# Output product of a pair of tiles by seven block products, transposed, in an attention and two-MLP kernel

## The chip, the cores and the metric

One core of a Trainium2 chip runs the whole program. The metric is device time in microseconds; lower is better. Engines are named as the profile names them: PE is the matrix engine (PEld its weight loads), DVE, ACT and POOL are the vector, scalar and GpSimd engines, SP issues all DMAs of this kernel from one queue, in order.

## What is computed

```python
def _attn_ref(q, k, v):
    ...
    attn = np.exp(scores)
    attn = attn / (np.sum(attn, axis=-1, keepdims=True) + 1e-09)
    return np.matmul(attn, v).astype(np.float32)

def _moe_ref(x, w_in, w_out, s, b):
    h = x @ w_in
    r = np.maximum(h, 0.0)
    g = s * (r * r) + b
    return (g @ w_out).astype(np.float32)

def _moe2_ref(x, w1, w2, w3, w_out):
    a = x @ w1
    b = x @ w2
    h = a * b @ w3
    return (h @ w_out).astype(np.float32)
```

Causal attention with a window of 128 (4 batches, 8 heads, 576 positions, head size 64) is followed by a first MLP (512 to 2048 to 512) and a second (512 to 1024, 1024 to 1024 to 512), over 2304 tokens, all in float32. Only the second MLP is touched by the change.

## The kernel before

Tokens are worked in six tiles of 384 (TT). Activations stand transposed, features on partitions and tokens along the free axis. A float32 matmul is made of three matmuls on rounded halves: each operand is split into a high part (an ACT copy to fp32r) and a low part (a subtraction), and `PASSES` runs high x high, high x low and low x high. `split_to` (line 624) is that split.

The program has these stages. Attention and the first MLP run interleaved over the six tiles (`slot`, line 983), and leave the second MLP's input x of every tile in DRAM (`x2d`, line 590). During the last tile of the first MLP, and behind it, three things are got ready:

- `w_chunk` (line 637) decodes the weights w1 and w2, eight chunks of 128 features, and builds seven left factors a chunk: A11, A12, A22, S1 to S4. Each is split and kept in SBUF, in the pool `wp` (34 buffers of 512 KB), until the end.
- `x_steps` (line 794) builds the right factors of the first pair of tiles: B11, B21, T1, T2, T4, B22, T3.
- `w3_unit` (line 595) multiplies w3 by the output weights, as these two have nothing between them: 8 steps j, each of 24 matmuls of 512 columns, into all eight PSUM banks; the weights come by `late_load` (line 1090). `w3_out` (line 607) evicts the eight banks, split, as `w3o`.

The last stage is the loop over three pairs of tiles (line 1137). `pair_chunk` (line 902) makes, for one chunk c, a and b of both tiles by seven block products instead of eight (Winograd's form of Strassen's method: rows are the chunk of w1 and that of w2, the inner axis is cut in two, columns are the two tiles). Each product (`prod`, line 831) is 6 matmuls of 384 columns. Sums are formed by `keep_copy` (ACT, line 843) and additions on DVE (lines 911, 924, 926, 928); the elementwise product a*b of the first tile is made on DVE (line 927) and that of the second on POOL (line 933). `p_split` (line 848) splits a product.

`out_mm` (line 868) is the output product: for each of the three 128-token blocks of a tile, 3 matmuls of 512 columns a chunk, accumulated over the eight chunks. The first tile's out_mm of chunk c-1 stands in the middle of chunk c:

```python
        u2 = keep_copy(u, gp, "r")
        if c:
            out_mm(2 * q, c - 1, p1s.pop())
            step()
```

and the second tile's eight stand after the pair's chunks, in one run of 72 matmuls with the first tile's last 9. Meanwhile `x_later` (line 737) builds the right factors of the next pair, a part at each `step()`, and stores them to DRAM; `x_fetch` (line 784) loads them all, 14 tiles of 384 KB, when a pair's chunks are done.

Order: a scheduler places instructions by priority (their order in the program) as operands and buffers come free, ahead of time; after that each engine runs its list in order. `tc.keep_in_program_order` holds marked instructions to the order of the program. A pool gives a tile the first buffer that is free, and the tile's first writer waits for the last reader of that buffer. Each DMA on SP also waits for the DMA eight places earlier.

## Time and profile before

| | us |
|---|---|
| median of 3 runs | 862.23 (862.08 to 874.1) |
| the profiled execution | 864.67 |
| its span | 862.8 |
| PE busy in the span | 854.9 |
| DVE busy | 571.8 |
| ACT busy | 496.5 |
| POOL busy | 344.0 |

The span is what the profiler saw from the first to the last instruction; the execution's own time is a little longer. Busy time of PE counts matmuls that overlap in the array, so it is not PE at its peak; the pitch of matmuls in a row says more.

### The profile page before, as it was taken

What the parts mean: (1) busy time and instruction counts of PE and PEld (TensorE: products, weight loads), DVE (VectorE), ACT (ScalarE), POOL (GpSimd) and SP (SyncE); (2) the same over time, 40 slices, a digit from 0 to 9 for tenths busy, and PEclk for the clock granted to TensorE, in tenths of its full rate; (3) what the DMA queues carried; (4) which work ended last, traced back from release to release, by engine and by line L of the source; (5) the groups of instructions that cost most, each with busy time, mean ns of one, the idle gap of its engine ahead of it and who ended that gap; (6) DMA issues with size and microseconds to landing.
All of it is one profiled execution on the core that took longest, in us unless ns stands there. A gap on an engine that the chain in (4) does not pass through costs nothing.

```text
span 862.8 us, 13636 instructions
## 1 busy us (share of the span) xinstructions
PE 854.9 (99%) x4676; PEld 777.4 (90%) x4676; DVE 571.8 (66%) x1186; ACT 496.5 (58%) x1180; POOL 344.0 (40%) x361
## 2 busy tenths in 40 slices
PE   9999999999999999999999999999999999999998
PEld 5766667999999999999999999889998999889996
DVE  5989997777878888778863998355544455333233
ACT  5777769877867777777764676343333334222222
POOL 0135457788666677666751302531111011101110
PEclk9999999999999999999999999999999999999999
DMA  9746513112354455445423577832428443610001
GB/s 335 284 175 213 211 60 106 55 55 85 113 167 163 163 165 197 168 155 165 135 98 119 169 268 271 312 116 83 153 86 311 147 156 120 257 73 1 1 1 74
DMA packets 51621, 129.10 MB, mean 150 GB/s; under 512 B 5984, under 2 KB 21600, under 8 KB 51552
## 3 DMA queue, kind: packets, MB, share of 16 engines
q1 hardware_dynamic: 51552, 128.23, 43.0%
q8 instruction: 37, 0.61, 0.3%
q14 instruction: 32, 0.26, 0.1%
HBM read 95.70 MB, written 32.51 MB: 149 GB/s over the span
## 4 chain that ended last, share of the span: by engine, by line
PE 89%; DVE 3%; ACT 3%; issue 2%; POOL 1%; DMA 1%; POOLq 0%; DVEq 0%; ACTq 0%; SPq 0%
PE acc L566 17%; PE hp L514 17%; PE oacc L876 12%; PE d L837 12%; PE u L837 9%; PE w3a L601 5%; PE acc L560 4%; PE hp L505 4%; PE pv L440 3%; PE s L310 2%; PE s L311 1%; PE s L305 1%; PE tp L387 1%; PE s L78 1%; PE xo L420 1%
## 5 line engine op out<-in xcount | busy, mean ns | idle before, releaser
L514 PE MATMUL hp<-x,w 128*128 128x384 f32 x960 | 185.7, 339 | 0.0
L514 PEld LDWEIGHTS hp<-x,w 128*128 128x128 f32 x960 | 167.3, 188 | 0.3
L566 PE MATMUL acc<-gh,w 128*128 128x384 f32 x640 | 125.9, 339 | 0.0
L933 POOL TENSOR_TENSOR p<-mc 128x384 f32<-128x384 f32 (+2 forms) x30 | 30.9, 1037 | 234.2 <-DVE mc L928 221.0
L566 PEld LDWEIGHTS acc<-gh,w 128*128 128x128 f32 x640 | 109.0, 188 | 0.6 <-ACT gh L535 0.3
L837 PE MATMUL d<-xb,wblk 128*128 128x384 f32 x576 | 107.9, 335 | 0.0
L837 PEld LDWEIGHTS d<-xb,wblk 128*128 128x128 f32 x576 | 101.2, 188 | 2.0
L403 POOL TENSOR_SCALAR_AFFINE_SELECT pt<-pp 128x768 fp32r<-128x768 f32 x80 | 79.0, 1010 | 31.0 <-PE pv L440 17.0
L876 PE MATMUL oacc<-w3o,ph 128*128 128x512 f32 x270 | 84.8, 395 | 0.0
L837 PE MATMUL u<-xb,wblk 128*128 128x384 f32 x432 | 83.6, 335 | 0.0
L272 POOL TENSOR_TENSOR kb<-qkraw,ka 128x512 fp32r<-128x512 f32 x40 | 57.4, 1435 | 58.7 <-ACT ka L271 58.3
L837 PEld LDWEIGHTS u<-xb,wblk 128*128 128x128 f32 x432 | 75.6, 188 | 0.9 <-ACT mc L845 0.6
L324 DVE CUSTOM_DVE_ANT_0 ns<-s,relm_sb 128x256 f32<-128x256 f32 (+1 forms) x144 | 53.3, 411 | 33.8 <-PE s L311 23.2
L368 POOL TENSOR_SCALAR pr<-pr,sm 128x128 f32<-128x128 f32 x90 | 45.5, 521 | 65.0 <-ACT z L150 20.6
L566 PE MATMUL acc<-gl,w 128*128 128x384 f32 x320 | 69.5, 337 | 1.3 <-DVE gl L543 1.3
L543 DVE TENSOR_TENSOR gl<-r,gh 128x384 fp32r<-128x384 f32 x80 | 57.3, 716 | 11.4 <-ACT gh L535 10.1
L924 DVE TENSOR_TENSOR mc<-d,mc 128x384 f32<-128x384 f32 x24 | 13.3, 556 | 76.4 <-PE d L837 76.4
L525 ACT ACTIVATE r<-hp 128x384 f32<-128x384 f32 x96 | 46.6, 485 | 25.3 <-PE hp L514 22.7
L845 ACT ACTIVATE mc<-d 128x384 f32<-128x384 f32 x48 | 23.6, 492 | 63.1 <-PE d L837 63.0
L876 PEld LDWEIGHTS oacc<-w3o,ph 128*128 128x128 f32 x270 | 50.4, 188 | 10.4
L347 ACT ACTIVATE pr<-pr,mn 128x128 f32<-128x128 f32 x120 | 46.9, 392 | 19.8 <-DVE pr L333 19.6
L566 PEld LDWEIGHTS acc<-gl,w 128*128 128x128 f32 x320 | 56.5, 188 | 1.7 <-DVE gl L543 1.6
(127 smaller groups left out, 1677.9 us busy)
## 6 DMA issues: line engine op xcount, KB each, us to landing
qkraw<-qk SPq DMA_DIRECT2D x40, 448.0 KB, 3.3
late<-st SPq DMA_DIRECT2D x23, 512.0 KB, 3.5
w<-late SPq DMA_DIRECT2D x23, 512.0 KB, 5.7
raw<-w_in SPq DMA_DIRECT2D x16, 512.0 KB, 6.5
raw<-w_out SPq DMA_DIRECT2D x16, 512.0 KB, 6.3
wr<-w SPq DMA_DIRECT2D x16, 512.0 KB, 4.1
st<-w3T SPq DMA_DIRECT2D x15, 512.0 KB, 3.8
xs<-x2d SPq DMA_DIRECT2D x32, 192.0 KB, 2.6
```

Of the source, the lines that this page charges most:

```text
L272: nc.gpsimd.tensor_tensor(out=kl, in0=k_r, in1=k.bitcast(F32), op=ALU.subtract)
L324: nc.vector.tensor_tensor_reduce(out=n[:, i, cs], in0=dst[i][:, cs], in1=relm_sb[:, VARIANT.get(t * NB + i, 0), cs], scale=2.0 ** -(h + 1) ...
L347: nc.scalar.activation(out=e[:, i, :], in_=e[:, i, :], func=AF.Exp, scale=-1.0, bias=mn[:, i:i + 1], accum_out=sm[:, i:i + 1],)
L368: nc.gpsimd.tensor_scalar(out=e[:, i, :], in0=e[:, i, :], scalar1=sm[:, i:i + 1], scalar2=1.0, op0=ALU.mult, op1=ALU.mult,)
L403: nc.gpsimd.affine_select(out=o[:, :, :, e, :], in_=pp.bitcast(F32), pattern=[[0, 2], [0, NB], [sign, P]], compare_op=op, fill=0.0, base=0 ...
L514: nc.tensor.matmul(out=hp, lhsT=wi[c][:, l, k * P:(k + 1) * P], rhs=xT[t, k][:, r, :], start=(n == 0), stop=(n == 3 * KD - 1),)
L525: chain(t * NC1 + c, nc.scalar.activation(out=rt[:, :TT], in_=hps.pop((t, c)), func=AF.Relu))
L543: nc.vector.tensor_tensor(out=gl, in0=rt[:, :TT], in1=gh.bitcast(F32), op=ALU.subtract)
L566: nc.tensor.matmul(out=x2acc[m], lhsT=wo[c][:, l, ms], rhs=g[r], start=(c == 0 and n == 0), stop=(c == NC1 - 1 and n == 2),)
L601: nc.tensor.matmul(out=accs[i], lhsT=w3g[i // 4, j][:, l, i % 4 * P:(i % 4 + 1) * P], rhs=wo2s[j][:, r, :], start=(j == 0 and n == 0), sto ...
L837: tc.keep_in_program_order(nc.tensor.matmul(out=dst, lhsT=w[:, l, ks], rhs=xblk[bnm, k][:, r, :], start=(start and n == 0), stop=(n == 5), ...
L876: tc.keep_in_program_order(nc.tensor.matmul(out=oacc[t, i], lhsT=p[l][:, cs], rhs=w3o[c][:, r, :], start=(c == 0 and n == 0), stop=(c == N ...
```

## The change

The output product is made transposed, features on partitions and the tokens of both tiles along the free axis, by seven block products a pair (`out_pair`). Its left factors come from the product of w3 and the output weights, built once by `w3_factors` in the first pair's chunks; its right factors are built from the products p of all eight chunks, which are kept for the pair (`p_tiles`). The output tensor is (512, 2304) and is turned on the host. Room in `wp` for this comes from the left factors of odd chunks, which are stored to DRAM and loaded again, a few at a time (`w_fetch`). The instructions of `w_chunk` are held to the program's order (`pin`).

```diff
@@ w3_out, w3_factors
+        for i in range(NC2):
+            z = w3z[i % (NC2 // 2)][:, i // (NC2 // 2), :]
+            if i % 2:
+                nc.vector.tensor_copy(out=z, in_=accs[i])
+            else:
+                nc.scalar.activation(out=z, in_=accs[i], func=AF.Copy)
+    def w3_factors():
...
+            tt(out=a22, in0=a21, in1=a22, op=ALU.add)
+            tt(out=a21, in0=a11, in1=a21, op=ALU.subtract)
+            tt(out=a11, in0=a22, in1=a11, op=ALU.subtract)
+            tt(out=a12, in0=a12, in1=a11, op=ALU.subtract)
+            for k, names in enumerate((("S2", "S3"), ("S4", "S1"))):
+                t = wp.tile([P, 2, DM], F32R, tag="w", name="w3f")
+                split_to((t[:, 0, :], t[:, 1, :]), z[:, k, :], nc.gpsimd)
...
@@ w_chunk
-            split_to((t[:, 0, :], t[:, 1, :]), src, lo_eng[0])
+            split_to((t[:, 0, :], t[:, 1, :]), src, lo_eng[0], pin)
...
+            if c % 2:
+                wfd[c, names] = dp.tile([P, 2 * DM], F32, name=f"wfd_{c}_{names[0]}")
+                nc.sync.dma_start(
+                    out=wfd[c, names], in_=t.rearrange("p a d -> p (a d)").bitcast(F32)
+                )
+                if c > 1:
+                    free_w[0] += 1
+    def w_fetch(c):
+        for (c_, names), d in wfd.items():
+            if c_ == c:
+                t = wp.tile([P, 2, DM], F32R, tag="w", name="wblk")
+                nc.sync.dma_start(out=t.rearrange("p a d -> p (a d)").bitcast(F32), in_=d)
...
@@ pair_chunk
-        u = pool.tile([P, TT], F32, tag=tag, name="u")
+        u, d, e, f = (pool.tile([P, TT], F32, tag=tag, name=k) for k in ("u", "d", "e", "f"))
+        prods[c] = p1, p2 = p_tiles(c)
...
-        if c:
-            out_mm(2 * q, c - 1, p1s.pop())
-            step()
+        step()
...
-        tt(out=m4, in0=m1, in1=m4, op=ALU.mult)
+        tt(out=p1, in0=m1, in1=m4, op=ALU.mult)
...
-        p1s.append(p_split([m4]))
...
+        nc.gpsimd.tensor_tensor(out=p2, in0=u2, in1=m5, op=ALU.mult)
@@ out_pair
+                if nm == "T1":
+                    tt(out=b11, in0=b12, in1=b11, op=ALU.subtract)
+                elif nm == "T2":
+                    tt(out=b11, in0=b22, in1=b11, op=ALU.subtract)
+                elif nm == "T4":
+                    tt(out=b21, in0=b11, in1=b21, op=ALU.subtract)
+                elif nm == "T3":
+                    nc.gpsimd.tensor_tensor(out=b12, in0=b22, in1=b12, op=ALU.subtract)
+                src = {"B21": b21, "T4": b21, "B22": b22, "T3": b12}.get(nm, b11)
+                y = xp.tile([P, 2, TT], F32R, tag="x", name="pf")
+                split_to((y[:, 0, :], y[:, 1, :]), src, nc.vector)
...
+                for k, (l, r) in enumerate(PASSES):
+                    tc.keep_in_program_order(nc.tensor.matmul(
+                        out=dst[m], lhsT=w[:, l, ms], rhs=ys[i][:, r, :],
...
+        y, y2 = factors("B11"), factors("B21")
+        product(u, "A11", y, True)
+        m1 = [keep_copy(x, gp, "r") for x in u]
+        y = factors("T1")
+        product(d, "A12", y2, True)
+        for m in range(2):
+            tt(out=m1[m], in0=d[m], in1=m1[m], op=ALU.add)
+            store(m1[m], 0, m, 2 * q)
+        y2 = factors("T2")
+        product(e, "S1", y, True)
+        m5 = [keep_copy(x, lp, "t") for x in e]
+        y = factors("T4")
+        product(u, "S2", y2, False)
+        u2 = [keep_copy(x, lp, "t") for x in u]
+        y2 = factors("B22")
+        product(f, "A22", y, True)
...
+        y = factors("T3")
+        product(e, "S4", y2, False)
...
+        product(u, "S3", y, False, True)
...
@@ the loop over pairs
+            pair_chunk(c, lambda: step(c))
+            if c % 2 and (c + 2 < NC2 or more):
+                w_fetch((c + 2) % NC2)
+        assert next(prep, None) is None and next(left, None) is None
         if more:
-            x_fetch(q + 1)
...
+            x_fetch(q + 1, FACTORS[:3])
+        out_pair(q, lambda: x_fetch(q + 1, FACTORS[3:]) if more else None)
```

How the lists of the engines change is shown at three places. The first is PE around the end of the last pair's chunks. `u`, `d`, `e`, `f` are the PSUM banks of a chunk's products, `oacc` and `ou`, `od`, `oe`, `of` those of the output product. Before, a chunk reads:

```order
L837 MATMUL d_7079<-xb,wblk 128x384 x6
L837 MATMUL u<-xb,wblk 128x384 x6
L876 MATMUL oacc<-w3o,ph 128x512 x2
L876 MATMUL oacc<-w3o,pl 128x512
L876 MATMUL oacc<-w3o,ph 128x512 x2
L876 MATMUL oacc<-w3o,pl 128x512
L876 MATMUL oacc<-w3o,ph 128x512 x2
L876 MATMUL oacc<-w3o,pl 128x512
L837 MATMUL d_7122<-xb,wblk 128x384 x6
```

Now, from the last chunk's last products on:

```order
L887 MATMUL f<-xb,wblk 128x384 x6
L887 MATMUL e<-xb,wblk 128x384 x6
L887 MATMUL u<-xb,wblk 128x384 x6
L963 MATMUL ou<-pf,w3f 128x384 x24
L963 MATMUL od<-pf,w3f 128x384 x24
L963 MATMUL oe<-pf,w3f 128x384 x24
L963 MATMUL ou<-pf,w3f 128x384 x24
L963 MATMUL of<-pf,w3f 128x384 x24
L963 MATMUL oe<-pf,w3f 128x384 x24
L963 MATMUL ou<-pf,w3f 128x384 x24
```

The output matmuls have left the chunks and stand in one run of 168 behind them.

The second place is DVE around the end of the last pair's chunks. `pl` and `pf` are split products and factors, `p` a product or the factor built over it, `mc` a kept sum. Before, from the last chunk's sums on:

```order
L926 TENSOR_TENSOR mc<-u,mc 128x384
L928 TENSOR_TENSOR mc<-u,mc 128x384
L927 TENSOR_TENSOR mc<-mc 128x384
L862 TENSOR_TENSOR pl<-mc,ph 128x384
L862 TENSOR_TENSOR pl<-p_8680,ph 128x256
L862 TENSOR_TENSOR pl<-p_8830,ph 128x128
L888 COPY ov<-oacc 128x512 x2
L862 TENSOR_TENSOR pl<-p_8830,ph 128x384 x2
```

Now, from the last chunk's sums on (line 927 makes the first of them, line 928 the product):

```order
L927 TENSOR_TENSOR mc<-u,mc 128x384
L929 TENSOR_TENSOR mc<-u,mc 128x384
L654 TENSOR_TENSOR pf<-p,pf 128x384 x2
L942 TENSOR_TENSOR p<-p 128x384
L928 TENSOR_TENSOR p<-mc 128x384
L654 TENSOR_TENSOR pf<-p,pf 128x384 x3
L944 TENSOR_TENSOR p<-p 128x384
L654 TENSOR_TENSOR pf<-p,pf 128x384
L944 TENSOR_TENSOR p<-p 128x384
L983 TENSOR_TENSOR mc<-od,mc 128x384
L654 TENSOR_TENSOR pf<-p,pf 128x384
L946 TENSOR_TENSOR p<-p 128x384
```

Where a few splits stood, splits and the subtractions of T1, T2 and T4 (lines 942, 944, 946) now stand close together.

The third place is SP in the stage of `w3_unit`. `late_16` to `late_22` are decoded weights of that stage, `raw` one that is still to be decoded, `wfd` the stored left factors, `xs` and `xfd` the next pair's x and its factors. Before:

```order
L1098 DMA w_6642<-late_18_5233 128x1024
L1098 DMA w_6676<-late_19_5371 128x1024
L1098 DMA w_6678<-late_20_5492 128x1024
L1098 DMA w_6680<-late_21_5604 128x1024
L1098 DMA w_6720<-late_22_5700 128x1024
L84 DMA raw_6722<-w3T 128x512
```

Now:

```order
L1168 DMA w_6670<-late_18_5233 128x1024
L794 DMA xs_6913<-x2d_2_2_98 128x384
L84 DMA raw_6771<-w3T 128x512
L1168 DMA w_6726<-late_19_5371 128x1024
L1168 DMA w_6728<-late_20_5492 128x1024
L1168 DMA w_6730<-late_21_5604 128x1024
L741 DMA wfd_7_A11_6711<-wblk_6708 128x1024
L1168 DMA w_6769<-late_22_5700 128x1024
```

An x load and the raw weights, whose buffer POOL's 16th split of the stage frees, moved ahead of late_19, and a store of left factors ahead of late_22.

## Rows read from the trace of the kernel before

**Rows 1.** The page, parts 1 and 4: busy time, and the chain by engine.

```profile
PE 854.9 (99%) x4676; PEld 777.4 (90%) x4676; DVE 571.8 (66%) x1186; ACT 496.5 (58%) x1180; POOL 344.0 (40%) x361
...
PE 89%; DVE 3%; ACT 3%; issue 2%; POOL 1%; DMA 1%; POOLq 0%; DVEq 0%; ACTq 0%; SPq 0%
```

**Rows 2.** Waits of PE, whole span, first two of six: us, times, longest us.

```profile
PE s L78 <- POOL zeros L950: 1.4, 1, 1.4
PE acc L566 <- DVE gl L543: 1.3, 1, 1.3
```

**Rows 3.** The chain in order of time, last stage: start us, length us, engine, tile.

```profile
586.70 2.08 PE d L837 x12
...
603.38 2.10 PE oacc L876 x9
...
655.79 18.88 PE oacc L876 x81
...
747.95 18.88 PE oacc L876 x81
...
840.14 18.89 PE oacc L876 x81
```

**Rows 4.** Windows: the w3 stage, the first pair's chunks, a burst of loads.

```profile
core 0: us, PE busy (x) PEld busy (x) DVE busy (x) ACT busy (x) POOL busy (x), PEclk, DMA share, GB/s
540.00:586.70 46.70, 46.70 (x216) 39.75 (x215) 21.69 (x30) 18.29 (x34) 20.46 (x18) 1.00 0.56 194
586.70:655.80 69.10, 69.10 (x376) 65.99 (x376) 34.51 (x65) 23.44 (x51) 9.06 (x9) 1.00 0.41 138
...
655.00:657.00 2.00, 2.00 (x11) 1.76 (x10) 1.53 (x4) 0.00 (x0) 0.01 (x1) 1.00 1.03 409
```

**Rows 5.** Groups by line and shape, 586 to 863 us: busy us, mean ns.

```profile
L845 ACT ACTIVATE mc<-d 128x384 f32<-128x384 f32 x48 | 23.6, 492 | 63.1 <-PE d L837 63.0
...
L862 DVE TENSOR_TENSOR pl<-mc,ph 128x384 fp32r<-128x384 f32 x24 | 17.0, 709 | 14.8 <-ACT ph L857 14.8
...
L857 ACT ACTIVATE ph<-p 128x384 fp32r<-128x384 f32 x15 | 7.8, 520 | 14.0 <-PE oacc L876 14.0
```

**Rows 6.** DVE in order of time: w_chunk's half-wide sums, then two chunks' ends.

```profile
494.60 0.41 DVE L693 TENSOR_TENSOR wr<-wr,z 128x256 f32<-128x256 f32 x1
...
610.79 0.84 DVE L862 TENSOR_TENSOR pl<-mc,ph 128x384 fp32r<-128x384 f32 x1 [0.59 <-ACT ph L857]
...
618.11 0.56 DVE L926 TENSOR_TENSOR mc<-u,mc 128x384 f32<-128x384 f32 x1 [0.47 <-PE u L837]
618.59 0.55 DVE L928 TENSOR_TENSOR mc<-u,mc 128x384 f32<-128x384 f32 x1
619.05 0.55 DVE L927 TENSOR_TENSOR mc<-mc 128x384 f32<-128x384 f32 x1
620.19 0.70 DVE L862 TENSOR_TENSOR pl<-mc,ph 128x384 fp32r<-128x384 f32 x1 [0.59 <-ACT ph L857]
```

**Rows 7.** POOL in order of time, at the same two chunks' ends.

```profile
609.81 1.40 POOL L933 TENSOR_TENSOR p<-mc 128x256 f32<-128x256 f32 x2 [8.19 <-DVE mc L928]
619.21 1.26 POOL L933 TENSOR_TENSOR p<-mc 128x384 f32<-128x384 f32 x1 [8.00 <-DVE mc L928]
```

**Rows 8.** POOL in order of time, w3 stage: splits of 384, 256 and 512.

```profile
539.49 1.04 POOL L626 TENSOR_TENSOR xb<-x2r,xb 128x384 fp32r<-128x384 f32 x1 [1.72 <-ACT xb L625]
...
548.61 0.74 POOL L626 TENSOR_TENSOR wblk<-z,wblk 128x256 fp32r<-128x256 f32 x1
...
551.37 1.29 POOL L626 TENSOR_TENSOR wblk<-z,wblk 128x512 fp32r<-128x512 f32 x1
```

**Rows 9.** DMA issues: count, KB each, median us from issue to landing.

```profile
w<-late SPq DMA_DIRECT2D x23, 512.0 KB, 5.7
...
xb<-xfd_T SPq DMA_DIRECT2D x16, 384.0 KB, 7.4
```

**Rows 10.** SP in order of time, w3 stage: the weights' loads.

```profile
550.13 10.97 SPq L1098 DMA_DIRECT2D w<-late  x7
```

More of the change, by code (lines that the diff above doesn't have):

```diff
@@ L655, in w_chunk @@
                 wf = raw.rearrange("p (n t) -> p n t", t=2)
[L656 removed]
+                pin(nc.scalar.activation(
+                    out=z, in_=wf[:, :, 1], func=AF.Copy, scale=2.0 ** -112
+                ))
             else:
[L658 removed]
+                pin(nc.scalar.activation(out=z, in_=raw[:, :DM], func=AF.Copy))
         yield 0
@@ L782, in x_later, with x_fetch @@
             yield
-    def x_fetch(q):
-        for nm in FACTORS:
+    def x_fetch(q, names):
+        for nm in names:
             for k in range(2):
@@ L868, in out_mm @@
-    def out_mm(t, c, p):
-        for i in range(NB):
-            if c == 0:
-                oacc[t, i] = (ps_rot if t % 2 else ps_acc).tile(
-                    [P, DM], F32, tag="rot" if t % 2 else "acc", name="oacc"
-                )
-            cs = slice(i * P, (i + 1) * P)
-            for n, (l, r) in enumerate(PASSES):
-                tc.keep_in_program_order(nc.tensor.matmul(
-                    out=oacc[t, i], lhsT=p[l][:, cs], rhs=w3o[c][:, r, :],
-                    start=(c == 0 and n == 0), stop=(c == NC2 - 1 and n == 2),
-                ))
-            if c == NC2 - 1:
-                if i == 2:
-                    z = lp.tile([P, DM], F32, tag="z3", name="ov", bufs=1)
-                else:
-                    z = zp.tile([P, DM], F32, tag="z", name="ov")
-                if i % 2:
-                    nc.scalar.activation(out=z, in_=oacc[t, i], func=AF.Copy)
-                else:
-                    nc.vector.tensor_copy(out=z, in_=oacc[t, i])
-                r0 = t * TT + i * P
-                nc.sync.dma_start(out=out[r0:r0 + P, :], in_=z)
@@ L892, in p2_parts, with p_tiles @@
-    def p2_parts(c):
-        out_, a = [], c * TT
-        while a < (c + 1) * TT:
-            i, e = a // (2 * DM), min((a // (2 * DM) + 1) * 2 * DM, (c + 1) * TT)
-            if i not in p2s:
-                p2s[i] = lp.tile([P, 2 * DM], F32, tag="raw", name="p2", bufs=3)
-            out_.append(p2s[i][:, a - i * 2 * DM:e - i * 2 * DM])
-            a = e
-        return out_
-    def pair_chunk(q, c, step):
+    def p_tiles(c):
+        if c < 3:
+            t = lp.tile([P, 2 * DM], F32, tag="raw", name="p", bufs=3)
+        elif c < 5:
+            return [gp.tile([P, TT], F32, tag=k, name="p") for k in ("gh", "gl")]
+        else:
+            t = wp.tile([P, 2 * DM], F32, tag="w", name="p")
+        return [t[:, :TT], t[:, TT:2 * TT]]
@@ L911, in pair_chunk @@
         tt(out=m1, in0=d, in1=m1, op=ALU.add)
-        e = ps_rot.tile([P, TT], F32, tag="rot", name="d5")
         prod(e, "S1", "T1", c, True)
@@ new lines, in out_pair, with factors, product, store @@
+    def out_pair(q, after):
+        tt = nc.vector.tensor_tensor
+        n = NC2 // 2
+        def factors(nm):
+            ys = []
+            for i in range(n):
+                (b11, b12), (b21, b22) = prods[i], prods[i + n]
+                if nm == "T1":
[9 more added lines that the diff above has]
+                split_to((y[:, 0, :], y[:, 1, :]), src, nc.vector)
+                ys.append(y)
+            return ys
+        def product(dst, wn, ys, start, outer=False):
+            loops = [(i, m) for i in range(n) for m in range(2)]
+            if outer:
+                loops.sort(key=lambda x: x[1])
+            for i, m in loops:
+                w, off = w3f[wn, i]
+                ms = slice(off + m * P, off + (m + 1) * P)
+                for k, (l, r) in enumerate(PASSES):
+                    tc.keep_in_program_order(nc.tensor.matmul(
+                        out=dst[m], lhsT=w[:, l, ms], rhs=ys[i][:, r, :],
+                        start=(start and i == 0 and k == 0), stop=(i == n - 1 and k == 2),
+                        skip_group_check=True,
+                    ))
+        def store(z, half, m, t):
+            r0 = (2 * half + m) * P
+            nc.sync.dma_start(out=out[r0:r0 + P, t * TT:(t + 1) * TT], in_=z)
+        d = [ps_rot.tile([P, TT], F32, tag="rot", name="od") for _ in range(2)]
+        u = [ps_rot.tile([P, TT], F32, tag="rot", name="ou") for _ in range(2)]
+        e = [ps_acc.tile([P, TT], F32, tag="acc", name="oe") for _ in range(2)]
+        f = [ps_acc.tile([P, TT], F32, tag="acc", name="of") for _ in range(2)]
+        y, y2 = factors("B11"), factors("B21")
[14 more added lines that the diff above has]
+        product(f, "A22", y, True)
+        m4 = [keep_copy(x, lp, "t") for x in f]
+        y = factors("T3")
+        product(e, "S4", y2, False)
+        for m in range(2):
+            tt(out=u2[m], in0=e[m], in1=u2[m], op=ALU.add)
+            store(u2[m], 0, m, 2 * q + 1)
+        product(u, "S3", y, False, True)
+        for m in range(2):
+            tt(out=m4[m], in0=u[m], in1=m4[m], op=ALU.subtract)
+            store(m4[m], 1, m, 2 * q)
+            tt(out=m5[m], in0=u[m], in1=m5[m], op=ALU.add)
+            store(m5[m], 1, m, 2 * q + 1)
+        after()
+        prods.clear()
```

110 lines of the change are left out of this document (48 added, 62 removed).

## The prediction

> **What bounds the kernel now.** I read the page first, then the chain of waits in order of time, then TensorE's own waits, and last the groups, DVE, POOL and DMAs of the last stage. The page shows TensorE (PE) busy 99% of the span and 89% of the chain that ended last on PE [rows 1]. A busy PE proves little by itself; TensorE's waits do: its six rows, of which the first two stand there, add up to 4.0 us of 862.8, and the lines in them are those of attention and the MLP, none of the last stage [rows 2]. So here time is the number of matmuls times their pitch. The chain gives both pitches [rows 3]: 12 matmuls of 384 columns take 2.08 us (0.1733 us each), 81 of 512 columns take 18.88 us (0.2331 us each). The same rows give the length of a pair: from one run of 81 to the next, 747.95 - 655.79 = 92.16 us, then 92.19.
>
> The granted clock is 1.00 in the windows of the last stage [rows 4], the full 2.4 GHz level, with PE never idle. I take no clock effect.
>
> **The change part by part.** *Output product.* Before, a pair costs 8 chunks x 7 products x 6 = 336 matmuls of 384 columns (58.24 us) and 2 tiles x 8 chunks x 9 = 144 of 512 columns (33.57 us). That is 91.81 of the 92.16; 0.35 is small waits. After, it is the same 336 and 7 x 24 = 168 more of 384 columns: 504 x 0.1733 = 87.36. If PE never waits, a pair is 92.16 - 87.36 = 4.80 us shorter, three pairs 14.4. Nothing else removes PE work, so about 848 is the floor (862.2 - 14.4). That is 1.7%, below the 2% which a measurement of this kernel can tell from no change.
>
> *What fed the output product, and what feeds it now.* Before, each of the 16 products p of a pair was split once (one ACT copy, one DVE subtraction), spread over the pair, beside at least 2.10 us of output matmuls. Now, in one run of 29.1 us, DVE issues 28 splits, 12 subtractions that build factors and 8 additions fed from PSUM; POOL issues 4 subtractions; ACT 28 copies and 8 evictions. PE takes 4.16 us for a product (24 x 0.1733). ACT is not the limit: 28 x 0.52 + 8 x 0.49 = 18.5 us [rows 5].
>
> DVE is. Call 0 the end of the last chunk's matmuls. The x pool has eight buffers, all held by x factors until the last chunk's own products free them, so the first split waits for S2*T2 (4 products before the end, so -3.1) and an ACT copy: about -2.65. The order of DVE then shows 34 instructions up to the last split of T2, the fourth factor: 16 splits, 12 subtractions, and the 6 of the last chunk and of the first output sums. The pitch on DVE in a row is 0.47 us (618.59 to 619.05, 618.11 to 618.59 [rows 6]), so 16.0 us. Beside them POOL runs five instructions. What that costs is in the rows: the split that starts at 620.19 while POOL works from 619.21 to 620.47 lasts 0.70 instead of the 0.55 of its neighbours, and the one at 610.79 lasts 0.84 and ends 0.42 after POOL [rows 6, 7]. A split that meets POOL therefore finishes 0.42 us after POOL does, whenever it began. POOL's instruction of 384 elements takes 1.04 alone and 1.26 behind DVE [rows 7, 8]; each takes about 0.9 us from DVE, five take 4.5. If every DVE instruction suffers, the 34th ends at -2.65 + 16.0 + 4.5 = 17.9. PE wants it at 3 x 4.16 + 3 x 1.04 + 0.17 = 15.8. That is 2.1 us late.
>
> The rows show held splits, whose two inputs lie in SBUF; none shows an instruction fed from PSUM beside POOL. The Trainium skill ("SBUF — State Buffer", Who interferes with whom) says that a DVE instruction with two SBUF inputs contends with POOL's reads, and one with a single SBUF input does not. The held splits agree with its first half. By the rule three of the 34 escape and the delay is nearer 1.5; it speaks against putting four POOL subtractions here in either case.
>
> I take 1.8 us per pair, 5.4 in all. After T2 there are only splits (12 in 12.5 us of PE), so DVE catches up and nothing more is lost. The bounds: 0, if POOL's share falls into DVE's idle time; and, if all 34 ran at the 709 ns that the splits beside POOL average [rows 5], -2.65 + 24.1 = 21.5, which is 5.7 late per pair.
>
> *The chunks without output matmuls.* A chunk shrinks from 9.4 to 7.28 us of PE. DVE needs five instructions for it (2.4 us) plus its share of the next pair's x factors (20 instructions over 6 chunks, 1.6 us). In the first pair come the output factors: on DVE 16 half-wide additions, 0.41 each [rows 6], and on POOL 4 x (0.74 + 3 x 1.29) = 18.4 us [rows 8], besides one product of 1.26 per chunk. A chunk of the first pair thus wants 4.8 us of DVE (2.4 + 1.6 + 0.8) and 3.6 of POOL (18.4 / 8 + 1.26), 8.4 in 7.28 if the two exclude each other, so over six chunks they fall 6 to 7 us behind. PE feels it only when a PSUM bank is wanted again, a whole chunk later, since u, d, e and f now alternate between two sets of four banks. I take 0.7 us, bounds 0 and 4.
>
> *Left factors of odd chunks.* Chunks 1, 3, 5 and 7 are stored once (12 x 512 KB) and fetched again (12 per pair). Fetches are issued on SP about two chunks ahead, some 14 us, and 512 KB lands in 5.7 us in a busy stretch [rows 9]. Per pair DMA then moves 6.3 MB of these, 8.6 MB of x loads and stores, 5.5 MB of x factors and 1.6 MB of output: 22 MB in 89 us, 250 GB/s, against 409 GB/s reached in the burst after a pair [rows 4]. It fits on average. The tight spot is the end of the output product: T2, T4, B22 and T3 of the next pair can be loaded only as their buffers come free, the last one at about 1 us after the product's end, needed 6.2 us after. Landing takes 7.4 us when 14 such loads stand in a row [rows 9], less here. I take 0.3 for each of two pair changes, bounds 0 and 2.
>
> *The stage before.* In the stage that multiplies w3 by w_out, SP's order now puts a load that waits for POOL's 16th split, and a store, ahead of the weights late_19 to late_22. Before, seven loads went out in a row from 550.13 to 561.1 [rows 10]. POOL's splits begin behind the last MLP eviction, about 544; 16 of them at 0.74 to 1.29 us with DVE in between end at 564 to 567. Unit 6 of 8 wants late_19 at 582.5 - 2 x 5.6 = 571.3 (24 matmuls of 512 columns are 5.6 us; 582.5 is the end of the stage, 674.67 less one pair of 92.16). With 4 to 5.7 us to land [rows 9] it is just in time. Stores also make the loads of that stage share the queue (194 GB/s before [rows 4]). I take 0.6, bounds 0 and 5. The eviction itself gets cheaper (one instruction per bank instead of two) but PE did not wait there. Holding the factors' order costs nothing that I can see: DVE's order there was already fixed.
>
> *The tail.* Two PSUM additions follow the last matmul instead of one copy: +0.3.
>
> **The sum.** -14.4 + 5.4 + 0.7 + 0.6 + 0.6 + 0.3 = -6.8 us. The profiled execution took 864.67 (span 862.8 and 1.9 around it), so 857.9 there; the median of the runs shown is 862.23, which gives 855.4. I say 855.5.
>
> **Rivals.**
> - *Everything is hidden.* DVE meets POOL in its idle time and the factors are always ready. For it: DVE is only 66% busy over the span, and about half busy in the last stage (34.5 of 69.1 us [rows 4]). Against it: half the subtractions fall in the first 16 us. Time 848 to 851, say 849.5.
> - *The factors set the pace of the output product, on the slower side.* Place: DVE between the last chunk and T2. If ACT's copy, which stands in the same queue behind evictions that wait for PE, hands over late each time, every split costs the 0.71 of the contended rows and PE waits 5.7 us per pair: -14.4 + 17.1 + 2.2 = +4.9, so 867. It decides from 4.8 us per pair, where it eats the whole gain. For it: each split is a hand-over ACT to DVE to PE with two sets of four buffers. Against it: in the stretch shown, DVE in a row holds 0.47.
> - *SP's queue holds weights back.* Loads behind instructions that wait for POOL come late, by 5 us in the w3 stage and 2 at each pair change: -6.8 + 4.4 + 3.4 = +1.0, so 863, no change. For it: SP is one queue in order, and each issue in it also waits for one eight places earlier. Against it: two chunks of lead.
> - *It doesn't do what it says*: if products had to be padded or the accumulators collided, PE's count would not be 168 per pair. The order shows exactly 24 per product, in 8 separate banks. I give it nothing.
>
> **How the numbers follow.** The forecast (852 to 860) 0.55, all hidden 0.2, slower by factors 0.14, held queue 0.11. The range from 849 to 868 takes in the hidden case's middle and the slower one's; outside is the floor at 848 and several bounds at once. Faster by over 2% would need under 845, 3 us under the floor: 0.02. Slower by over 2% needs 879.5, all bounds together (-14.4 + 17.1 + 4 + 4 + 5 + 0.3 = +16, 878) or a wait I don't see: 0.04. Within 2%: 0.94.
>
> **What would show it.** In the profile after, matmuls of the last stage all at 0.173 us pitch; PE waits for the tile pf, on DVE or ACT, concentrated in the second and the fourth output product, 1 to 3 us per pair; POOL's p subtractions beside DVE splits of over 0.7 us; pairs 88 to 90 us apart. PE waits in the chunks on u, in the first pair only, under 2 us. I am wrong if PE waits for DMA (wblk, xb or late weights) by more than 3 us in all, if waits on pf exceed 4.8 us per pair, or if a pair is under 87.5 us.

## The result, and the profile after

The changed kernel takes 871.46 us (median of 6 runs, 867.71 to 872.44), the kernel before 862.15 beside it: ratio 1.0103, 95% interval 1.0091 to 1.0116. It is slower by one per cent; 855.5 was forecast, and the range of 849 to 868 does not hold it. The profiled execution took 871.33 (span 869.6).

First, where each pair's chunks and its output product begin (PE's timeline: start, duration, engine, line, operation, tiles, count), to be set beside [rows 3]:

```profile
580.05 1.23 PE L887 MATMUL u<-xb,wblk 128*128 128x384 f32 x6
...
643.73 1.55 PE L963 MATMUL ou<-pf,w3f 128*128 128x384 f32 x8
...
674.40 1.20 PE L887 MATMUL u<-xb,wblk 128*128 128x384 f32 x6
...
740.72 1.55 PE L963 MATMUL ou<-pf,w3f 128*128 128x384 f32 x8
...
771.39 1.20 PE L887 MATMUL u<-xb,wblk 128*128 128x384 f32 x6
...
834.71 1.55 PE L963 MATMUL ou<-pf,w3f 128*128 128x384 f32 x8
```

The pairs take 94.35, 96.99 and (to the last matmul's end at 865.66) 94.27 us, against 92.16 and 92.19 before. At 0.1733 us a matmul, a pair's chunks need 58.24 and its output product 29.12. So the chunks lose 5.4, 8.1 and 5.1 us, together 18.6, and the output products 1.55, 1.55 and 1.83, together 4.9. That closes the account of the two profiled executions: -14.4 of work, +18.6, +4.9, +0.1 at the tail (3.9 us behind the last matmul), and -2.45 because the last stage began at 580.05 instead of 582.5: +6.75, against a measured 871.33 - 864.67 = +6.66. The start of that stage lay between 579.7 and 582.9 in the kernels below too, and no run shows why. The profiled execution of the kernel before took 2.5 us more than its median; against the medians, 871.46 - 862.15 = +9.3, the first three terms and the tail alone give +9.2, so the 2.45 may belong to that one execution. (One of the kernels below, e1, has a profiled execution that was disturbed in its first 290 us; its last stage, which is used below, starts 20 us later and ran at clock 1.00.)

Next, what TensorE waited for (us in total, times, longest), where [rows 2] had nothing of the last stage:

```profile
PE u L887 <- ACT mc L895: 7.7, 7, 1.8
PE u L887 <- DMA xb<-xfd_T: 4.2, 3, 1.5
PE w3a L601 <- DMA w<-late: 1.8, 2, 1.6
...
PE od L963 <- ACT pf L653: 1.0, 3, 0.4
PE od L963 <- DVE pf L654: 0.8, 3, 0.3
PE e L887 <- ACT mc L895: 0.7, 1, 0.7
...
PE e L887 <- DMA xb<-xfd_B: 0.3, 1, 0.3
```

The waits on pf are those that I had forecast. The first two rows are not. `mc` is ACT's copy of a PSUM bank inside a chunk, `xfd_T` and `xfd_B` the x factors T and B of the next pair. The copies cost 4.1 us in the first pair and 4.3 in the second.

How the copy comes late, in the third chunk of the second pair (timelines of ACT, DVE, POOL and PE; in brackets the idle time before, and what ended it):

```profile
693.73 0.56 DVE L810 TENSOR_TENSOR xs<-xs 128x384 f32<-128x384 f32 x1 [1.39 <-DMA xs<-x2d]
694.32 0.53 ACT L653 ACTIVATE xh<-xs 128x384 fp32r<-128x384 f32 x1 [3.15 <-DVE xs L810]
695.14 0.55 DVE L810 TENSOR_TENSOR xs<-xs 128x384 f32<-128x384 f32 x1
695.36 1.17 POOL L930 TENSOR_TENSOR p<-mc 128x384 f32<-128x384 f32 x1 [7.66 <-DVE mc L929]
695.60 1.35 DVE L928 TENSOR_TENSOR p<-mc 128x384 f32<-128x384 f32 x1
695.77 0.52 ACT L653 ACTIVATE xh<-xs 128x384 fp32r<-128x384 f32 x1 [0.92 <-DVE xs L810]
697.04 0.49 ACT L895 ACTIVATE mc<-u 128x384 f32<-128x384 f32 x1 [0.76 <-DVE p L928]
697.59 1.33 PE L887 MATMUL u<-xb,wblk 128*128 128x384 f32 x6 [1.75 <-ACT mc L895]
```

S2*T2 (697.59) adds onto bank u, so it waits until ACT has copied u's first product. That copy wants a buffer `r`, which the product p1 of the chunk before (695.60) still reads; p1 stands on DVE behind two subtractions for the next pair's x factors (693.73, which waited for a load, and 695.14), and is held by POOL besides. ACT has two x copies ahead of its copy of u too. There was next to no room: the bank's last product of the chunk before ends at 693.76, PE comes back for S2*T2 2.1 us later, and the sums m4 and m5, p1 and the copy alone take 0.47 + 0.47 + 0.55 + 0.49 = 2.0 us.

At a pair change, the loads (SP's timeline) and the matmuls that want them:

```profile
772.01 0.82 SPq L838 DMA_DIRECT2D xb<-xfd_T  x1
772.92 1.07 SPq L971 DMA_DIRECT2D out_dram<-mc  x2
774.10 0.40 SPq L838 DMA_DIRECT2D xb<-xfd_T  x1
...
779.40 0.41 PE L887 MATMUL u<-xb,wblk 128*128 128x384 f32 x1 [1.46 <-DMA xb<-xfd_T]
781.18 3.75 PE L887 MATMUL u<-xb,wblk 128*128 128x384 f32 x11 [1.37 <-DMA xb<-xfd_T]
```

The last T3 is issued at 774.10, 2.7 us after the product's end, behind two output stores that wait for DVE. And from the first of the 11 matmuls behind the gap (781.18) to the next product (784.76) it is 3.58 us, where 11 x 0.1733 is 1.91. The windows say why (PE busy, granted clock, DMA share, GB/s):

```profile
778.00:779.00 1.00, 0.00 (x0) 1.00 0.54 207
...
782.00:783.00 1.00, 1.00 (x5) 0.50 0.00 0
...
785.00:786.00 1.00, 1.00 (x7) 1.00 0.79 311
```

After the gap the granted clock is 0.50, the 1.2 GHz level, until about 784.6. Against [rows 4] that is new. It cost 1.7 us here. The runs of the changed kernel had a mean clock of 0.994 to 0.998 over the span; the missing share of 870 us is 2 to 5 us, an estimate of what the clock cost in them.

### The profile page after: what moved, and what is told of

It is laid out like the page before. It is cut to its first block, busy times and chain, and to the rows that moved or that the text cites. A ratio compares the mean times of both kernels' runs of the same rounds, so it can differ in the third digit from the quotient of the medians.

```text
span 869.6 us, 14147 instructions
## 1 busy us (share of the span) xinstructions
PE 846.0 (97%) x4748; PEld 782.1 (90%) x4748; DVE 633.9 (73%) x1276; ACT 522.7 (60%) x1240; POOL 375.9 (43%) x383
## 4 chain that ended last, share of the span: by engine, by line
PE 78%; DVE 8%; DMA 5%; ACT 4%; issue 2%; POOL 1%; SPq 1%; DVEq 0%; ACTq 0%; POOLq 0%
PE hp L514 19%; PE acc L566 19%; PE u L887 7%; PE e L887 4%; PE acc L560 4%; PE hp L505 4%; PE pv L440 4%; PE oe L963 3%; PE ou L963 2%; PE d L887 2%; PE f L887 2%; DMA xb<-xfd_T 2%; DVE pf L654 2%; PE s L310 2%; PE s L311 2%
## 5 line engine op out<-in xcount | busy, mean ns | idle before, releaser
L930 POOL TENSOR_TENSOR p<-mc 128x384 f32<-128x384 f32 x24 | 29.1, 1213 | 174.9 <-DVE mc L929 164.2
L887 PE MATMUL u<-xb,wblk 128*128 128x384 f32 x432 | 86.5, 342 | 11.9 <-ACT mc L895 7.7
L895 ACT ACTIVATE mc<-u 128x384 f32<-128x384 f32 x48 | 23.5, 489 | 85.6 <-DVE p L928 41.5
L887 PE MATMUL e<-xb,wblk 128*128 128x384 f32 x288 | 58.2, 335 | 1.0 <-ACT mc L895 0.7
L654 DVE TENSOR_TENSOR pf<-p,pf 128x384 fp32r<-128x384 f32 x84 | 48.4, 613 | 11.2 <-ACT pf L653 10.9
L887 PEld LDWEIGHTS e<-xb,wblk 128*128 128x128 f32 x288 | 50.5, 188 | 1.8 <-ACT mc L895 1.0
L530 ACT ACTIVATE r<-r 128x384 f32<-128x384 f32 x96 | 49.8, 520 | 1.6
L925 DVE TENSOR_TENSOR mc<-e,mc 128x384 f32<-128x384 f32 x24 | 13.3, 555 | 48.0 <-PE e L887 44.2
```

What stands on the lines that cost most here:

```text
L530: chain(t * NC1 + c, nc.scalar.activation(out=rt[:, :TT], in_=rt[:, :TT], func=AF.Square))
L654: pin(eng.tensor_tensor(out=dst[1], in0=src, in1=dst[0].bitcast(F32), op=ALU.subtract))
L887: tc.keep_in_program_order(nc.tensor.matmul(out=dst, lhsT=w[:, l, ks], rhs=xblk[bnm, k][:, r, :], start=(start and n == 0), stop=(n == 5), ...
```

## The experiments

Lost time per pair, as above: chunks over 58.24 us, output product over 29.12, in each profiled execution. Ratios are to the kernel before, run beside.

| run | ratio [95%] | chunks lose, pairs 1, 2, 3 | output loses |
|---|---|---|---|
| changed kernel | 1.0103 [1.0091, 1.0116] | 5.4, 8.1, 5.1 | 1.5, 1.5, 1.8 |
| e1 | 1.0083 [1.0066, 1.0099] | 5.1, 7.3, 2.0 | 1.6, 1.6, 1.9 |
| e2 | 1.0119 [1.0101, 1.0138] | 5.8, 10.4, 3.7 | 1.5, 1.5, 1.7 |
| e3 | 1.0086 [1.0069, 1.0103] | 6.7, 9.5, 0.0 | 1.6, 1.6, 1.9 |
| e4 | 1.0088 [1.0065, 1.011] | 5.5, 7.3, 2.6 | 1.6, 1.6, 1.9 |
| e5 | 0.9967 [0.9939, 0.9996] | 0.9, 4.4, 1.9 | 1.6, 1.7, 1.8 |
| e6 | 1.0209 [1.0167, 1.0251] | 3.1, 7.3, 5.3 | 5.6, 6.1, 6.0 |
| e7 | 1.0099 [1.0065, 1.0134] | 6.3, 8.8, 2.6 | 1.9, 1.9, 2.1 |
| e8 | 1.0177 [1.0102, 1.0252] | 8.0, 10.9, 2.3 | 1.6, 1.6, 1.9 |
| e9 | 0.9948 [0.9914, 0.9982] | 0.9, 4.1, 0.3 | 1.6, 1.7, 1.9 |
| e10 | 1.0253 [1.0149, 1.0356] | 13.6, 13.3, 0.2 | 2.1, 2.2, 2.4 |
| e11 | 1.0059 [1.0024, 1.0094] | 5.9, 5.9, 0.0 | 2.1, 2.1, 2.4 |
| e12 | 1.0009 [0.9986, 1.0032] | 6.8, 2.8, 0.0 | 1.6, 1.6, 1.8 |
| e13 | 1.0003 [0.999, 1.0016] | 2.7, 2.5, 0.7 | 2.1, 2.1, 2.3 |
| e14 | 0.998 [0.9969, 0.9991] | 6.3, 1.4, 0.3 | 2.1, 2.1, 2.3 |
| e15 | 0.996 [0.9944, 0.9976] | 5.1, 1.1, 0.2 | 1.6, 1.7, 1.8 |
| e16 | 0.9915 [0.9892, 0.9938] | 0.9, 0.0, 0.2 | 1.6, 1.7, 1.8 |

**e1 and e2: other buffers for the late copies.**

```diff
-        m1 = keep_copy(u, gp, "r")
+        m1 = keep_copy(u, lp, "t")
...
-        m4 = keep_copy(f, lp, "t")
+        m4 = keep_copy(f, gp, "r")
```

e1 makes this edit in `pair_chunk`, e2 the same one in `out_pair`.

> The changed kernel with two buffers exchanged inside a chunk: the copy of u after the first product goes to the six buffers t, the copy of f after the fifth goes to the two buffers r. Changed kernel: 871.5 us (ratio to the kernel before 1.0103). Theory A (held buffers: the first copy of a chunk waits for a buffer r until DVE and POOL have read it for the products p of the chunk before, and S2*T2 waits for that copy): TensorE's waits on the copy in the chunks, 8.4 us in all, go to under 2; time 863 to 866. Theory C (traffic: the fetched left factors and the x loads make everything land late): the same copies are late for another reason, time 869 to 872. Theory D (DVE and POOL exclude each other): the splits stay as slow, time 869 to 872.

> The changed kernel with the same exchange in the output product alone: the copies of ou after its first product go to buffers t, the copies of of after its fifth go to buffers r. Theory A: ACT, which in the profile waits 5.2 us there with its copies for the splits queued behind, does not stop, TensorE's waits on pf (1.8 us) and the slow fourth product (4.69 instead of 4.32 us, each pair) go; time 867 to 869. Theory D, on which my prediction stood: the factors are late because POOL's subtractions hold DVE's splits; nothing changes, 871 to 872, and the output product keeps its 30.7 us instead of 29.1.

Theory A fails in both. In e1 TensorE still waits 6.7 us for the copies of u and the first pair loses 5.1: taken off the buffers r, the copy stands behind x copies in ACT's list, and in turn for a buffer t. So the buffers r alone are not the cause. In e2 the copies of ou wait for PE alone and end 2.3 us before ACT starts the split that PE wants, and the output product is unchanged, so its 1.5 us is not ACT's held copy either.

**e3: loads first.**

```diff
-        product(u, "S3", y, False, True)
+        product(u, "S3", y, False, q + 1 == NTILE // 2)
+        after()
         for m in range(2):
...
-        after()
```

> The changed kernel with the loads of the next pair's T2, T4, B22 and T3 issued ahead of the last four stores of the output, and, but for the last pair, the last output product taken factor by factor, so that the buffers come free 1.5, 1 and 0.5 us sooner. Theory B (the last x factor is issued too late, behind stores that wait for DVE): it is issued about 2 us sooner, TensorE's waits on xb, 4.5 us in all, fall to under 1.5; time 867 to 869. Theory C: the loads are held by the bandwidth, land as late as before, 870 to 872.

The third pair's chunks lose 0.0 instead of 5.1: B holds there. In the eight kernels that leave these loads as they were, the third pair loses 1.9 to 5.3; in the nine that issue them first, 0.7 at most. So B is worth 2 to 5 us at this change. The last T loads now go out together, ahead of the stores, and S4*B22 and S3*T3 follow without a gap:

```profile
773.14 1.36 SPq L838 DMA_DIRECT2D xb<-xfd_T  x2
774.59 2.07 SPq L971 DMA_DIRECT2D out_dram<-mc  x4
...
779.15 1.20 PE L887 MATMUL e<-xb,wblk 128*128 128x384 f32 x6
780.19 2.24 PE L887 MATMUL u<-xb,wblk 128*128 128x384 f32 x12
```

But the second pair loses more, 9.5: the waits on xb went, and waits on ACT's copies took their place (8.3 us for u, 1.8 for e).

**e4: no left factor stored or fetched.**

```diff
-        w, off = wblk[a, c]
+        w, off = wblk[a, c - c % 2]
```

with the stores and `w_fetch`'s loads taken out.

> The changed kernel with no left factor stored or fetched: the odd chunks multiply with the factors of the even chunk before them, which leaves out 12 stores and 30 fetches of 512 KB (all work on the engines stays). Theory C: with this traffic gone the waits on xb, the late x loads and the two waits of the stage before (1.8 us) go: 861 to 865. Theories A and B: the copies and the last x factor are held by other things, at most the 1.8 us of the stage before and 1 to 2 us of landing times go: 868 to 871.

The first two pairs lose 5.5 and 7.3, nearly as much as before: theory C, that the new traffic delays everything, falls for the chunks. The third pair's 2.6 lies within the spread just given. The waits for late weights in the stage before do not go either (2.3 us against 1.8), so the stores of left factors are not what delays them.

**e5: x factors without their arithmetic.**

```diff
-                split_to((z.bitcast(F32R), r.bitcast(F32R)), r, nc.vector)
...
-            nc.vector.tensor_tensor(out=out, in0=a, in1=b, op=ALU.subtract)
+            pass
```

> The changed kernel with the making of the next pair's x factors reduced to its transfers: the same 16 loads and 28 stores per pair, but none of the 14 copies on ACT and 20 subtractions on DVE per pair (what is stored is not the factors). Theory E, formed after the first four runs: this work is a chain (load, subtract, split, store, buffer free for the next load) that takes about 8 us a step by the issues of its loads (679.3, 689.0, 697.0, 706.3, 711.7, 721.5), a chunk is now 7.28 us, and its instructions stand ahead of the chunk's copies and products in the in-order lists of ACT and DVE, so its waits become PE's. By E the chunks of the first two pairs (which lose 5.4 and 8.1 us) lose under 1 and about 5 (the pair change), time 862 to 864. Theory C (transfers): the chunks lose the same, 869 to 872.

This is the largest single cause: 5.4 goes to 0.9 in the first pair and 8.1 to 4.4 in the second, with all the transfers still there. It is 36 short instructions a pair (14 copies, 22 subtractions; the expectation, like the prediction, counts two too few) in two in-order lists, not the transfers by themselves. e5 takes these instructions out, so it can't tell their place in the lists from the time they take; e8, e10, e11, e13 and e14 move them.

**e6 and e7: the output product.** e6 puts p1's multiplication next to m4's and holds it there, with `keep_in_program_order` also on the factors from B21 on; e7 is one line:

```diff
-                    nc.gpsimd.tensor_tensor(out=b12, in0=b22, in1=b12, op=ALU.subtract)
+                    tt(out=b12, in0=b22, in1=b12, op=ALU.subtract)
```

> The changed kernel with DVE's order held in two places: in a chunk the sum m4 and the product p1 stand next to each other, ahead of the sum m5; in the output product the factors from B21 on stand behind the last chunk's p1. Nothing is left out. Theory F (the output product loses its 1.55 us because p1 of the last chunk stands behind eight instructions of the factors): 0.5 or less lost there, three times 1 us; in the chunks a part of the held copies goes; 866 to 868. Theory D (POOL holds DVE, whatever the order): the output product still takes 30.7 us, 870 to 872.

> The changed kernel with the four subtractions of T3 of the output product on DVE instead of POOL. Theory D, as in my prediction (each POOL instruction takes 0.9 us from DVE ahead of the second and fourth product): the output product falls from 30.7 to about 29.3 us, time 867 to 868. Theory F: DVE's list is the same ahead of p1 but without the holds, at most half of the loss goes; 869 to 871.

Neither kernel gains, but each shows a part of the cause. In e6 the second product runs without a gap, in all three pairs; so what it lost came from what stands ahead of p1 on DVE: the first factors' instructions and POOL's holds on them. With the factors held in order, each output product now loses 6 us further on, where ACT and DVE hand over one piece of a factor after the other and PE waits most in the third product:

```profile
645.37 4.32 PE L965 MATMUL od<-pf,w3f 128*128 128x384 f32 x24
...
PE oe L965 <- DVE pf L654: 3.4, 6, 0.8
```

In e7 four of POOL's holds a pair go and the product still gets 0.3 us longer. DVE did gain: p1 ends 6.1 us after the product's start (649.87 + 0.56 - 644.32) where it was 7.2 (650.35 + 0.55 - 643.73). But now its split waits on ACT, behind a copy of ou whose buffer POOL's product p2 has to free, and p2 takes 3.54 us instead of 1.26 while DVE runs one instruction with both inputs in SBUF after the other (ACT and POOL, e7):

```profile
651.34 0.49 ACT L895 ACTIVATE mc<-ou 128x384 f32<-128x384 f32 x1 [6.35 <-POOL p L930]
647.76 3.54 POOL L930 TENSOR_TENSOR p<-mc 128x384 f32<-128x384 f32 x1 [8.11 <-DVE mc L929]
```

That is the held copy of e2, which cost nothing while p1 was later. So POOL's holds are 1.1 us of what p1 was late, and the factors' instructions ahead of it the rest. Only e6 takes both away from p1, and it pays further on.

**e8: x steps spread over eight chunks** (a step at products 4, 13, 22, 31, 40 and 49 of the pair instead of one in each of chunks 1 to 6).

> The changed kernel with the steps of the next pair's x factors 9 products apart over all eight chunks (9.4 us) instead of one in each of chunks 1 to 6 (7.28 us). Theory E: the loads have landed and the stores have freed their buffers when a step comes, ACT and DVE no longer wait for them, and the chunks of the first two pairs lose 1 to 3 and 5 to 6 us instead of 5.4 and 8.1; 866 to 868. If it is not the pace but merely where the instructions stand (some steps now fall ahead of a copy that PE waits for): 870 to 874.

The second alternative, and worse: 8.0 and 10.9 us, ratio 1.0177. More time for the chain does not help while its instructions fall ahead of a copy that PE waits for.

**e9: e3 and e5 in one kernel.**

> The runs e3 and e5 together: loads of the next pair ahead of the last stores, and the making of the x factors reduced to its transfers (its copies and subtractions are left out). If theories B and E are the two causes of what the chunks lose, the chunks of all three pairs lose under 1 us, what is left is the output product's 1.6 us per pair, TensorE's clock stays at 1.00 for lack of gaps, and the time comes to 853 to 857, about what I had predicted for the whole change. If a third cause holds the chunks (left factors or x factors late), 858 to 862.

One gap is left, at the start of the second pair (ACT and PE; lines left out of a kernel shift its numbers, L889 is `keep_copy`, L881 `prod`):

```profile
679.48 0.49 ACT L889 ACTIVATE mc<-e 128x384 f32<-128x384 f32 x1 [2.37 <-DMA out_dram<-mc]
680.02 2.29 PE L881 MATMUL e<-xb,wblk 128*128 128x384 f32 x6 [2.40 <-ACT mc L889]
```

So two causes are not enough (the second pair still loses 4.1), and the time, 859.59, lies where the expectation put a third. The copy of e waits until an output tile has been written to DRAM: it takes its turn among six buffers t with output tiles and x tiles. That is the third cause, G. The matmuls behind the gap ran at clock 0.50 (680 to 683), which makes 2.4 us into 4.1.

**e10 and e11: the x steps behind the products, held there.** Both with e3's edit and m4, p1, m5 held in this order:

```diff
             pair_chunk(c, lambda: step(c))
+            if c < NC2 - 2:
+                next(prep, None)
```

e10 makes the x copies on DVE (`pin(nc.vector.tensor_copy(...))`), e11 on ACT.

> A version with nothing left out: loads first as in e3; the product p1 next to m4 on DVE; the x factors' steps behind the products of chunks 0 to 5, held there, and their copies on DVE instead of ACT, so that ACT has none of this work in its list. Theory E: ACT's copies no longer wait for x loads, DVE has from 1.4 to 6.2 us of a chunk for the step, and the chunks lose under 1 us in the first pair and under 2 in the second; 855 to 860. If DVE's own list (the first copy's buffer r waits for p1 on DVE) is as bad as ACT's: 864 to 868.

> As the run before, but the copies of the x factors' splits stay on ACT. Theory E, in the form that ACT's list is what counts: ACT still stands waiting for x loads ahead of the chunk's first copy, 863 to 867, 4 or more above the run before. If only the place on DVE counts, the two are alike within 1.5 us.

e10 went the wrong way, though its lists were as wanted. Its waits of ACT and PE tell why:

```profile
ACT mc L901 <- DMA xfd_T<-xs: 11.1, 5, 2.6
ACT mc L901 <- DMA xfd_B<-xs: 10.2, 6, 3.6
...
PE e L893 <- ACT mc L901: 14.8, 5, 3.7
```

The chunk's copies stand 21 us for buffers t whose x tiles are on their way to DRAM. e11, with its x copies on ACT, came out at 869.12: above its range, and under e10 instead of over it, so taking the x copies off ACT is not by itself a gain.

**e12 to e14: the buffers t divided**, two (k) for the chunk's copies, four for x tiles; e12 with e3's edit alone, e13 on e11, e14 on e10.

```diff
-        m5 = keep_copy(e, lp, "t")
+        m5 = keep_copy(e, lp, "k")
...
-        m4 = keep_copy(f, lp, "t")
+        m4 = keep_copy(f, lp, "k")
```

> Nothing left out: loads first as in e3, and the six buffers t, which the copies of e and f in a chunk shared with the x loads in turn, divided: two (k) for these copies, four (t) for the x loads. Theory G, formed after e9 to e11: where DVE's and ACT's lists are mended, the copy of e waits for a buffer t until an x tile or an output tile has been written to DRAM (up to 2.7 us in the profile of e11, 2.4 at the pair change of e9), and S4*B22 for that copy. Here the lists are not mended, so by E the first pair loses as before, about 5 to 6 us; the second pair loses 2 to 3 us less than the 9.5 of e3 (no wait for output tiles at its start); time 866 to 868.

> Nothing left out: e11 (loads first, p1 next to m4, the x steps behind the products of chunks 0 to 5, their copies on ACT) with the six buffers t divided as in e12. Theory G: the waits for tiles on their way to DRAM (10.8 us of ACT's, three of PE's four gaps in the chunks) go, the first two pairs lose 1 to 3 us each instead of 5.9, and the time is 858 to 862, under the kernel before or level with it. If the x chain itself (8 us a step) holds the lists, the pairs lose 4 to 6 and the time stays at 866 to 868.

> As e13, with the copies of the x factors on DVE as in e10. Theory G: e10's waits were those for t (21 us of ACT's), so the pairs fall from 13 us lost to 2 to 4; 860 to 864. Theory E alone: DVE, with 13 more instructions and its own copy waiting for p1, stays behind by much, 870 or more.

G holds. Same memory, other turns: e10's 1.0253 becomes 0.998, its 13.3 us in the second pair 1.4, and the row of 14.8 us is gone; what is left in e14's chunks is 3.9 us of waits for copies of u, all in the first pair, which loses 6.3, more than expected. e12 shows that dividing alone brings the second pair from e3's 9.5 to 2.8, more than expected, while the first pair stays at 6.8. And from e12 to e13 only the place of the x steps and the held orders change, and the first pair's 6.8 becomes 2.7: there the place of this work counts, not only its amount.

**e15: the best of them, nothing left out.** e13 with the x copies on ACT in the first pair and on DVE in the second, and m4, p1, m5 held in chunks 0 to 6 only.

> Nothing left out: e13 with two changes. The copies of the x factors stay on ACT in the first pair (where DVE and POOL also make the output factors, e13 loses 2.7 us there and e14 6.3) and go to DVE in the second (e13 2.5, e14 1.4); and the order m4, p1, m5 is held in chunks 0 to 6 only, since in the last chunk it cost the output product 0.5 us a pair (e11, e13, e14: 31.2 against 30.7). By these numbers e13's 862.9 less 1.1 less 1.5 is 860.3; 859 to 861.5, ratio to the kernel before 0.996 to 0.999.

859.28 us, ratio 0.996 [0.9944, 0.9976]: faster than both kernels, as expected in sum. By pairs it is less tidy: the first lost 5.1 instead of 2.7 (one gap of 2.5 us before S4*B22, with the clock at 0.50 behind it). e13 had this gap too, 2.2 us long, and the clock did not fall. In both, the copy of e stands on ACT behind x copies that wait for an x load: theory E.

**e16: all three causes out.**

> All three causes taken out at once: loads first, the making of the x factors reduced to its transfers (its copies and subtractions left out), the buffers t divided. If B, E and G are the whole of what the chunks lose, the chunks lose under 1 us in each pair, the clock stays at 1.00, the output product keeps its 1.6 us, and the time is 854 to 857, what my sum gave for the change. If the chunks still lose 2 us or more in a pair, a fourth cause is left (held r buffers, left factors late).

855.17 us, ratio 0.9915 [0.9892, 0.9938]. TensorE's waits in the last stage are those on pf, and one of 0.3 us:

```profile
PE od L959 <- ACT pf L653: 1.1, 3, 0.4
PE od L959 <- DVE pf L654: 0.8, 3, 0.3
...
PE u L883 <- ACT mc L891: 0.3, 1, 0.3
```

So the three causes account for all but 1.1 of the 18.6 us that the chunks lost. Two pairs of kernels differ by one cause alone, with the others out: e9 and e16 by the divided buffers (second pair 4.1 to 0.0), e12 and e16 by the x factors' arithmetic (6.8 to 0.9 and 2.8 to 0.0). (e16 does not compute the x factors; e15 does, and pays.)

## Why the prediction was wrong

**Right: the work.** A chunk without waits takes 7.28 us and an output product's piece 4.16, as counted. With the causes out, e16 comes to 855.17 where the sum gave 855.5; but it lacks the x factors' arithmetic, which the sum had.

**Right: the output product.** 4.9 us lost against 5.4 forecast, in the second and the fourth product as said. The sum had put it all on the fourth, on the last split of T2; the second loses 1.2 of it and the fourth 0.4:

```profile
647.89 3.29 PE L963 MATMUL od<-pf,w3f 128*128 128x384 f32 x18
651.50 0.44 PE L963 MATMUL od<-pf,w3f 128*128 128x384 f32 x1 [0.32 <-ACT pf L653]
652.23 1.16 PE L963 MATMUL od<-pf,w3f 128*128 128x384 f32 x5 [0.29 <-DVE pf L654]
...
657.39 4.69 PE L963 MATMUL ou<-pf,w3f 128*128 128x384 f32 x24
```

The piece that is late first is p1 of the last chunk, a step that the sum did not price by itself. Here POOL meets DVE, and the trace now has what I could not see before, an instruction fed from PSUM beside POOL:

```profile
645.19 1.20 POOL L948 TENSOR_TENSOR p<-p 128x384 f32<-128x384 f32 x1 [1.49 <-DVE p L942]
645.44 1.36 DVE L942 TENSOR_TENSOR p<-p 128x384 f32<-128x384 f32 x1
646.94 1.20 POOL L948 TENSOR_TENSOR p<-p 128x384 f32<-128x384 f32 x1 [0.56 <-DVE p L942]
647.19 0.54 DVE L927 TENSOR_TENSOR mc<-u,mc 128x384 f32<-128x384 f32 x1
```

With both inputs in SBUF it takes 1.36 instead of 0.55; with one from PSUM, 0.54 in the midst of POOL's. The Trainium skill ("SBUF — State Buffer", Who interferes with whom) says just this; the trace agrees, and the 1.5 a pair that I had worked out by that rule is nearer to the measured 1.55 than my 1.8. In part that is luck: POOL's five instructions took about 2.8 us from DVE where the sum had 4.5 (0.8 for each of three, 0.3 for another, against e7's unheld splits), and DVE waited 0.6 us for ACT where it had nothing.

**The step that failed: "the chunks without output matmuls", +0.7.** I found DVE and POOL 6 to 7 us behind in the first pair and wrote that PE feels it "only when a PSUM bank is wanted again, a whole chunk later". The bank was not the first thing wanted. S2*T2 wants the copy of u three products into the next chunk, the copy wants a buffer that p1 frees on DVE, and the copies of e and f want turns among buffers with x and output tiles. Before, 2.1 us of output matmuls stood in each chunk just where the x step's instructions come; in that time or soon behind it ACT and DVE did them. In one chunk of the second pair of the kernel before, for example, DVE is done with the x work and waits 2.24 us for PE before it makes the chunk's last sums:

```profile
699.84 0.56 DVE L924 TENSOR_TENSOR mc<-d,mc 128x384 f32<-128x384 f32 x1 [2.24 <-PE d L837]
```

That the output matmuls made this room is argued from the order of the program; no run put them back. I subtracted the matmuls without asking what they covered. The first pair's chunks lost 5.4 us where my 0.7, with a bound of 4, stood for it, and I had put nothing for the second. e5 prices the x work in the lists at 4.5 us in the first pair and 3.6 in the second; with the other causes out (e12 against e16) it is 5.9 and 2.8. What I had named as a sign of being wrong came: PE waits for DMA, 6.3 us of the rows above, more than 3.

**Also failed: the pair changes, 0.3 each, bounds 0 and 2.** I had the place (the last x factors, needed 6.2 us after the product's end) and trusted the landing time. What I missed is the order on SP: the last load stands behind stores that wait for DVE, and goes out 2.6 to 2.7 us after the end, not 1. With the third cause behind it and the clock, the changes cost 4.4 us in the second pair (e5, which e16 brings to 0.0) and 5.1 in the third (e3; in other kernels as little as 1.9). Of the rivals the held SP queue was nearest, priced at 2 a change.

**Failed: no clock effect.** True of the last stage of the kernel before, which has no gaps; the changed one makes them.

**The stage before**: 1.8 us of waits for late weights, forecast 0.6, within its bounds of 0 to 5; the load of late_19 went out at 563.3, behind the one that waits for POOL, where I had 564 to 567. The tail: 0.1 for 0.3.

## What to carry to other kernels

When work is taken off the engine that bounds, list each hand-over inside the shortened stretch (who copies, into which buffer, who frees it, what else stands in that engine's list) and recount its slack; average load of the helpers does not show it. Copies that the bounding engine waits for should not take turns for buffers with tiles that go to or come from DRAM: dividing six buffers into two and four was worth over 20 us in one version (e10 to e14). And remove causes together before giving one up: the loads first (e3, 869.41) left the time within 0.3% of the changed kernel, because the next wait took its place, though they were worth up to 5 us in the third pair; and e7's earlier p1 gained nothing for the same reason.

## What I had not expected of the hardware

A gap of under 2 us can halve TensorE's clock, and the same gap need not. In the changed kernel and in e3, PE waits 1.76 us at the same place, and only in e3 do the next matmuls run at half pace (e3 first, with a window of PE busy, granted clock, DMA share and GB/s):

```profile
600.11 1.57 PE L887 MATMUL u<-xb,wblk 128*128 128x384 f32 x6 [1.76 <-ACT mc L895]
601.47 2.12 PE L887 MATMUL f<-xb,wblk 128*128 128x384 f32 x6
...
601.00:602.00 1.00, 1.00 (x5) 0.50 0.92 329
```

```profile
600.22 1.34 PE L887 MATMUL u<-xb,wblk 128*128 128x384 f32 x6 [1.76 <-ACT mc L895]
601.40 1.20 PE L887 MATMUL f<-xb,wblk 128*128 128x384 f32 x6
```

The Trainium skill ("TensorE: Matmul & The Clock Gate", The HAM clock gate) knows the two levels, and that idleness brings the lower one; the granted clock of 0.50 in the rows agrees. Such a fall cost 1.5 to 1.7 us here (e3 at 600, e9 at 680, the changed kernel at 781), about as much as the gap itself, and it adds to the spread of one kernel's runs: e16's ran from 853.75 at a mean clock of 1.000 to 860.22 at 0.992. It is not all of the spread: e15's 861.94 had 1.000, its 858.55 only 0.997.
